# q and k' turned in 32x32 squares by VectorE and carried to their lanes, in place of transposing transfers

## The chip, the cores and the metric

One core of one Trainium2 chip. The metric is the device time of one execution in microseconds, the median of three runs: 465.61 us for the kernel before (465.29 to 465.65).

## The reference

A Linformer attention followed by a feed-forward layer. Batch 8, 8 heads, 1024 tokens, 64 channels a head, projected length 64:

```python
k_proj = np.einsum('ks,bhsd->bhkd', E, k)
v_proj = np.einsum('ks,bhsd->bhkd', F, v)
scores = scale * np.matmul(q, k_proj.transpose(0, 1, 3, 2))
attn = softmax(scores)                      # max subtracted, sum + 1e-09
attn_out = np.matmul(attn, v_proj)
...
x = attn_out.transpose(0, 2, 1, 3).reshape(B * S, H * D)   # 8192 x 512
h = x @ w_in                                # 512 x 2048
out = (h * (1.0 / (1.0 + np.exp(-1.702 * h)))) @ w_out     # 2048 x 512
```

## The kernel before

The 8192 tokens are worked in 16 blocks of 512, two to a batch: block j belongs to batch j // 2. TensorE multiplies with its operands standing on lanes: for the scores of a block it needs q with the 64 channels of a head on the lanes (two heads fill 128), and the projected k, called k', in the same way. q comes from memory with tokens on the lanes, so it has to be transposed; the projection gives k' with the projected index on the lanes, so it has to be transposed too.

Batch 0 is transposed on TensorE against an identity in the opening (`q_tr0`, `q_tr`, `k_tr`). From batch 1 on the kernel before lets a transfer do it. `q_dma` (L234 to L240; steps `qd`, `qda`, `qdb`) issues on SyncE's queue (SP) one transposing transfer of q_sb into qT for a whole batch, or half a batch in the opening; the step `kd` (L684) does the same from k_b into kt. k_b is the copy of k' out of PSUM (`kb`, L682).

The two matmuls of the feed-forward layer are each done in 7 products of half size instead of 8 (Winograd's form of Strassen's scheme): steps `u0` to `u3` make the first (L610), with sums of halves on VectorE (`xs`, `d1`, `d2`) and gelu on ScalarE (`g11` and so on, L626); `F1` to `F7` make the second (L504), from sums `gs` of the gelu outputs (L374), with copies `Fc`, `Fo` and sums `Fd` to the output tile. Eight PSUM banks are shared by all of it by a fixed plan.

The order of the work is written out by hand as words. `OPEN` lists the opening up to block 4, `STEPS` is one steady step j (run for j = 4 to 12), `TAIL` the end. A word `sc.1+3` in STEPS is the step "scores, second half" for block j + 3, `name@n/D` in OPEN the step for block n with its copy on VectorE (D) or ScalarE (A). Each engine takes its instructions in the order in which the words come, and waits in that order. Words named in BATCH are done only for the first block of a batch.

The words that matter here: `pj` projects k and v of a batch (L674). `kb` and `vq` copy the results. `sc` makes scores (L249), `ex` their exponentials (L638), `su`, `den`, `ga`, `rc`, `sr`, `sb` the sums, their reciprocals and their spreading over lanes by transfers through DRAM (den, rc, rdr, rbc), `va` the product with v', `mv` its scaling into xT (L646). `st0`, `st1` store the output. `ld` has GpSimd (POOL) issue the loads of k and v of the next batch into their single buffers, `lq` that of q of the next batch, eight transfers into the single buffer q_sb. Both first do a tiny copy into `held` that reads a tile whose arrival shall hold the loads back: for `ld` (L677) it reads qT of the batch, for `lq` (L696) it reads rbc. In a steady step the order on SP is: gather of den, transposition of k', a store, rdr, both rbc pieces, transposition of q, the other store.

Of the kernel before, what the change touches and what calls it, by code (L numbers as in the profile page):

```python
# [17 lines left out]
def kernel(ctx, tc, q, k, v, E, F,  # L18
# [86 lines left out]
    kts = [consts.tile([P, HP, KP], BF16, name=f"kt{i}") for i in range(2)]  # L105
# [89 lines left out]
    def k_tr(k_b, p0):  # L195
        n = k_b.shape[1] // 2
        t_ps = f_tile([P, n, KP], BF16)
        for p in range(n):
            nc.tensor.transpose(t_ps[:, p, :], k_b[:, 2 * p:2 * p + 2, :].rearrange("k t d -> k (t d)"),
                                ident[:KP, :KP])  # L200
        nc.vector.tensor_copy(kts[0][:, p0:p0 + n, :], t_ps)
# [21 lines left out]
    def q_tr(g):  # L223
        def go():
            if 0 not in qT:
                qT[0] = att.tile([P, J, HP, P], BF16, name="qT")
            t_ps = f_tile([P, 2, HP, P], BF16)
            for jj in range(2):
                for p in range(HP):
                    nc.tensor.transpose(t_ps[:, jj, p, :],  # L230
                                        qt[0][:, 2 * g + jj, 2 * p:2 * p + 2, :].rearrange("s t d -> s (t d)"), ident)
            nc.vector.tensor_copy(qT[0][:, 2 * g:2 * g + 2], t_ps)
        return go

    def q_dma(b, j0=0, n=J):
        def go():
            if j0 == 0:
                qT[b] = att.tile([P, J, HP, P], BF16, name="qT")
            nc.sync.dma_start_transpose(out=qT[b][:, j0:j0 + n].rearrange("r j p s -> r (j p) s"),
                                        in_=qt[b][:, j0:j0 + n].rearrange("s j h d -> s (j h d)"))  # L240
        return go

    def eight(outs, lhsTs, rhss, w=32):


        for i, ro in ((0, (LO, HI)), (1, (HI, LO))):
            for c in range(0, KP, w):
                for ri, r in zip((LO, HI), ro):
                    nc.tensor.matmul(outs[i][r.start + c:r.start + c + w], lhsTs[i][ri, c:c + w], rhss[i][ri],  # L249
                                     start=True, stop=True)  # L250

    def scores0(u, half):
# [4 lines left out]
        eight(s_ps, [kts[0][:, 2 * u + i, :] for i in range(2)], [q0s[half][u][:, :, i, :] for i in range(2)], KP)  # L257
# [118 lines left out]
    def ffn2_ops(j):  # L376
# [8 lines left out]
        wi.5@1/D sc.1@1:5,6 sc.0@1:7,4 ex.0.0@1 ex.1.1@1 ex.0.1@1 O.2.0@0:3 O.3.0@0:2 O.2.1@0 tk.0.1@1:0 qda@2  # L385
        O.3.1@0 ex.1.0@1 tk.0.0@1:5 tr.0.1@1 tm.0.1@1 tk.1.0@1:0 tk.1.1@1:7 tr.0.0@1 tm.0.0@1 O.1.0@0:6 O.1.1@0
        O.1.2@0 xt.0@1:4 gt@6 tr.1.0@1 tk.3.0@1:1 tr.1.1@1 tm.1.1@1 O.3.2@0 O.3.3@0 tk.2.1@1:5 tk.2.0@1:7
        xc.0@1/A wi.4@1 O.1.3@0 tm.1.0@1 tr.2.0@1 xt.1@1:0 tm.2.0@1 oc.3@0/D ws.1@1 tr.3.0@1 xc.1@1/A O.0.0@0:7
        ws.0@1 O.0.1@0 O.2.2@0 tk.3.1@1:4 tr.2.1@1 tm.2.1@1 O.0.2@0 tm.3.0@1 tr.3.1@1 tm.3.1@1 oc.1@0/D xt.2@1:5
        xc.2@1/A O.0.3@0 xt.3@1:1 xc.3@1/A O.2.3@0 ws.2@1 L.5@1:0 L.0@1:6 oc.0@0/D L.15@1:2 Lg.0@1 oc.2@0/A  # L390
        Lg.5@1 gt@3 L.4@1:4 L.1@1:7 pj@2:5 Lg.4@1 L.14@1:0 kb@2/A Lg.15@1 L.11@1:1 Lg.14@1 Lg.1@1 kd@2 L.2@1:6
        L.7@1:4 ws.3@1 L.9@1:3 vx.0@2 vq.0@2/D vx.1@2 vq.1@2/D Lg.7@1 Lg.11@1 ws.4@1 qdb@2 Lg.9@1 L.6@1:5
        L.8@1:4 L.10@1:7 Lg.8@1 Lg.2@1 L.3@1:1 L.12@1:3 L.13@1:2 ws.5@1/D lq@2 Lg.10@1 Lg.3@1 Lg.6@1 Lg.12@1
        Lg.13@1 gs1.0@1 sc.1@3:3,6 sc.0@2:0,1 gs2.0@1 sc.0@3:4,7 F1.0@1:2 ex.1.1@3 ex.0.1@2 gs1.1@1 gs4.0@1
        F1.1@1 gs2.1@1 gs3.0@1 Fc1@1:1/D F5.0@1:5 ex.1.0@3 ex.0.1@3 F5.1@1 F6.0@1 ex.0.0@3 ex.0.0@2 su@3:0,6
        den.0@3/A sc.1@2:3,4 tk.0.0@2:7 F2.1@1 ex.1.0@2 tk.1.0@2:0 ex.1.1@2 Fc3@1/A den.1@3/D tr.0.0@2 tm.0.0@2
        gs4.1@1 tk.0.1@2:3 tr.1.0@2 tm.1.0@2 tr.0.1@2 tm.0.1@2 tk.1.1@2:7 tr.1.1@2 F2.0@1 tm.1.1@2 F6.1@1 s0.1@0
        tk.2.1@2:4 tk.2.0@2:0 xt.0@2:6 s0.0@0 xt.1@2:3 F3.1@1 tr.2.1@2 tr.2.0@2 xc.0@2/A tm.2.0@2 tm.2.1@2 ga@3
        gs3.1@1 tk.3.0@2:0 F3.0@1 xc.1@2/A tk.3.1@2:6 tr.3.0@2 Fc2@1/A xt.2@2:3 tm.3.0@2 xc.2@2/A tr.3.1@2
        tm.3.1@2 gt@4 Fo0@1/A rc@3 xs.0@2 Fd2@1 F7.1@1 u0.P1@2:7 u0.c1@2:5/D xt.3@2:3 u1.P5@2:6 u1.P1@2:0  # L400
        u1.c1@2:2/D F7.0@1 xc.3@2/A xs.1@2 u0.P2@2 Fd1@1 u0.P5@2:4 u0.c3@2/D sr@3 u1.P2@2 u0.P6@2 u1.P6@2 F4.0@1
        u1.c3@2/D u0.c2@2/D u1.P3@2 ld@2 u2.P1@2:3 u0.g11@2 u3.P1@2:7 xs.2@2 u1.c2@2/A qd@4 u1.P7@2 u1.d2@2
        u1.g11@2 xs.3@2 F4.1@1 u0.P3@2 u1.g12@2 u2.c1@2:0/A sb@3 u1.d1@2 u2.P2@2 u0.d2@2 Fo1@1/A u3.c1@2:6/A
        u0.P7@2 u3.P2@2 u3.P5@2:4 u2.P5@2:1 u3.P6@2 u2.P6@2 u0.d1@2 u1.g22@2 u3.c3@2/D u3.P3@2 u3.g11@2 u0.g22@2
        u0.g12@2 pj@4:7 u3.c2@2/A u2.c3@2/A gs1.0@2 u3.P7@2 u2.g11@2 u3.d2@2 u2.c2@2/D gs3.0@2 gs2.0@2 u2.P7@2
        u1.P4@2 u3.g12@2 u2.P3@2 kb@4/A u3.d1@2 u0.P4@2 kd@4 u2.d1@2 F1.0@2:3 u1.g21@2 u2.d2@2 F1.1@2 u2.g22@2
        u3.g22@2 u2.g12@2 vq.1@4/A u0.g21@2 gs1.1@2 u3.P4@2 u2.P4@2 vq.0@4/A Fc1@2:1/A u3.g21@2 u2.g21@2
        va.1@3:2,7 va.0@3:4,5 gs2.1@2 mv.1.0@3 mv.0.0@3 F6.1@2 F2.0@2 mv.0.1@3 xs.0@3 mv.1.1@3 F2.1@2 sc.1@4:4,5
        sc.0@4:2,0 F6.0@2 ex.1.1@4 xs.1@3 gs3.1@2 Fc2@2/D F5.0@2:7 st1@1 st0@1 Fo0@2/D ex.0.1@4 ex.0.0@4
        ex.1.0@4 F5.1@2 F7.1@2 sc.0@5:3,6 sc.1@5:0,5 ex.0.0@5 su@4:4,2 den.1@4/A gs4.0@2 F7.0@2 ex.0.1@5  # L410
        den.0@4/D Fc3@2/D u0.P1@3:2 u1.P5@3:3 u0.P5@3:4 ex.1.0@5 u0.c1@3:6/A u1.P1@3:0 u0.c3@3/A gs4.1@2 xs.2@3
        u0.P6@3 Fd1@2 u0.c2@3/D F3.0@2 u1.c3@3/D ex.1.1@5 gt@2 ga@4 u1.c1@3:5/D u0.P3@3 F3.1@2 Fd2@2 u1.P6@3
        gt@5 u0.d2@3 rc@4 u1.c2@3/A ld@4 u0.P2@3 xs.3@3 u1.P2@3 u0.P7@3 u0.g11@3 F4.1@2 u1.P3@3 u1.P7@3 u0.d1@3
        u0.P4@3 u2.P1@3:7 F4.0@2 u1.d2@3 su@5:4,3 sr@4 u1.g11@3 pj@6:0 u1.d1@3 sb@4 Fo1@2/D u3.P1@3:2 u1.g12@3
        u1.P4@3 den.0@5/A u1.g22@3 u0.g22@3 den.1@5/D u2.c1@3:3/A u0.g12@3 kb@6/D u2.P6@3 u0.g21@3 gs1.0@3
        gs2.0@3 u2.P5@3:1 u3.P5@3:6 u3.c1@3:4/A vq.0@6/A u2.c3@3/A u3.c3@3/D u3.P6@3 u2.P2@3 u2.c2@3/A u2.P3@3
        gs3.0@3 vq.1@6/A u3.c2@3/A u3.P3@3 u2.g11@3 lq@4 u2.d2@3 u3.P2@3 u3.g11@3 u2.P7@3 u1.g21@3 u3.d2@3
        u3.P7@3 u3.d1@3 u3.g12@3 u2.g12@3 va.0@4:2,0 va.1@4:1,6 u2.d1@3 mv.0.1@4 mv.0.0@4 u2.g22@3 u3.g22@3
        F1.0@3:5 F1.1@3 u3.P4@3 kd@6 u3.g21@3 ga@5 gs1.1@3 u2.P4@3 mv.1.0@4 u2.g21@3 Fc1@3:1/A gs2.1@3 mv.1.1@4
        u1.P1@4:7 F5.0@3:0 u1.c1@4:6/A qd@6 xs.0@4 F5.1@3 rc@5 F6.1@3 F2.1@3 F2.0@3 u1.P2@4 u1.g11@4 F6.0@3  # L420
        sc.0@6:7,3 sc.1@6:4,2 ex.1.0@6 st1@2 xs.1@4 sr@5 u1.P6@4 xs.2@4 st0@2 xs.3@4 gs3.1@3 gs4.1@3 Fc3@3/D
        sb@5 gs4.0@3 ex.1.1@6 F3.0@3 F3.1@3 u1.c2@4/A Fc2@3/D Fo0@3/D ld@6 ex.0.0@6 F7.0@3 u1.P5@4:4 F7.1@3
        u1.P7@4 u2.P1@4:7 u1.c3@4/D ex.0.1@6 u0.P1@4:2 u1.P3@4 u0.P5@4:5 u0.c1@4:3/A gt@7 Fd1@3 Fd2@3 u0.P6@4
        u1.d2@4 u3.P1@4:0 u0.c3@4/D u0.c2@4/D u3.c1@4:4/A u0.P2@4 u1.g12@4 u0.P3@4 u0.g11@4 u0.d2@4 F4.0@3
        u3.P6@4 F4.1@3 u3.P2@4 u1.d1@4 u3.c2@4/D gt@1 u3.g11@4 u0.P7@4 Fo1@3/A u0.d1@4 u1.g22@4 u0.g22@4
        u2.P5@4:2 u1.P4@4 u2.c1@4:5/D u3.P5@4:0 u3.P7@4 u3.c3@4/D u2.P6@4 u1.g21@4 u0.g12@4 u2.c3@4/A u0.P4@4
        u3.d1@4 u3.P3@4 u3.P4@4 u2.c2@4/D u0.g21@4 u2.P2@4 u3.g21@4 u2.g11@4 u3.d2@4 u2.P7@4 u2.P3@4 va.0@5:0,3
        su@6:1,4 den.0@6/A u2.d1@4 den.1@6/A u2.g22@4 mv.0.1@5 u2.d2@4 va.1@5:6,7 u2.P4@4 u3.g12@4 gs1.0@4 lq@6
        u2.g21@4 st0@3
# [368 lines left out]
```

## Time and profile before

| | |
|---|---|
| median of three runs | 465.61 us |
| the profiled execution | 464.02 us |
| its span, first to last instruction | 462.2 us |
| DVE busy | 343.6 us (74%) |
| ACT busy | 307.8 us (67%) |
| POOL busy | 82.5 us (18%) |
| transfers issued by POOL (queue 0) | 86,496 packets, 29.37 MB |
| transfers issued by SP and ACT (queue 1) | 47,108 packets, 38.90 MB |
| transposing transfers of q | 8, issue 2.0 to 10.4 us (median 7.7), landing 9.1 to 14.2 us after issue |
| transposing transfers of k' | 7, issue 1.18 to 1.52 us, landing 2.9 to 6.6 us after issue |
| loads of k, v (1 MB each as they land) | median 12.2 and 16.2 us from issue to landing |

The profile is one execution, with times in microseconds from the span's start. PE is TensorE's matmuls, DVE is VectorE, ACT ScalarE, POOL GpSimd, SP SyncE. Line numbers are those of the kernel before. In a timeline row the columns are start, time (of all merged instructions), engine, line, operation, output from input, shape, count, and in square brackets how long the engine stood idle just before and what ended that wait. In the slices each digit is the busy share of a fortieth of the span in tenths; PEclk is the clock that TensorE was granted. Time that an engine other than TensorE idles costs nothing by itself.

### The profile page before, as it was taken

The numbers are of one execution on the slowest core, as the hardware profiler recorded it, in microseconds if no ns is written. First come the engines' busy times: TensorE is split into PE (matmuls) and PEld (weight loads), VectorE is DVE, ScalarE is ACT, GpSimd is POOL, SyncE is SP. The second block draws the span as 40 slices with busy tenths as digits, with TensorE's granted clock in tenths as the row PEclk, the third lists the DMA queues.
The fourth block names the chain that finished last, engine by engine and source line by source line (L and its number), as shares of the span: only waits on it lengthen the run. The fifth ranks groups of instructions, "written<-read, shape, count | busy, mean of one in ns | idle before, by whom it ended". The sixth has DMA issues, their size and how long they took to land.

```text
span 462.2 us, 10631 instructions
## 1 busy us (share of the span) xinstructions
PE 455.6 (99%) x4378; PEld 361.9 (78%) x4378; DVE 343.6 (74%) x616; ACT 307.8 (67%) x539; POOL 82.5 (18%) x111
## 2 busy tenths in 40 slices
PE   8999999999999999999999999999999999999997
PEld 4644448877778788887888788787888888888886
DVE  4547957887785977878687876888788796977771
ACT  2665367686767967769585776958677676737462
POOL 7463107052013201041010601015000000000000
PEclk9999999999999999999999999999999999999999
DMA  9999999999999978999988987989664123242022
GB/s 167 200 187 207 182 174 156 197 241 199 148 219 254 158 145 135 223 127 157 162 152 188 156 126 143 211 158 155 138 128 116 45 79 88 94 94 92 1 91 92
DMA packets 133731, 69.19 MB, mean 150 GB/s; under 512 B 98484, under 2 KB 123060, under 8 KB 133684
## 3 DMA queue, kind: packets, MB, share of 16 engines
q0 software_dynamic: 86496, 29.37, 56.7%
q1 hardware_dynamic: 47108, 38.90, 34.5%
q8 instruction: 34, 0.56, 0.5%
q10 hardware_dynamic: 80, 0.26, 0.2%
q14 instruction: 13, 0.11, 0.1%
HBM read 72.88 MB, written 16.99 MB: 194 GB/s over the span
## 4 chain that ended last, share of the span: by engine, by line
PE 87%; DMA 8%; DVE 2%; POOL 1%; issue 1%; ACT 0%; SPq 0%; DVEq 0%; POOLq 0%; ACTq 0%
PE k_ps L504 39%; PE k_ps L610 35%; PE k_ps L249 3%; PE k_ps L550 3%; PE k_ps L556 3%; DMA v_sb<-in_v_dram 3%; PE k_ps L674 2%; DMA w_in_sb<-in_moe_w_in_dram 2%; DMA rbc<-rdr 2%; DMA rdr<-rc 1%; DVE sg L357 1%; PE k_ps L652 1%; POOL k_sb L58 0%; POOL v_sb L58 0%; PE k_ps L567 0%
## 5 line engine op out<-in xcount | busy, mean ns | idle before, releaser
L504 PEld LDWEIGHTS <-sg 128*128 128x128 bf16 x960 | 93.6, 98 | 12.0 <-issue 1.3
L610 PEld LDWEIGHTS <-late 128*128 128x128 bf16 x896 | 87.4, 98 | 11.3 <-issue 1.2
L489 DVE TENSOR_TENSOR q_even<-k_ps,q_even 128x512 f32<-128x512 f32 x112 | 74.6, 687 | 22.7 <-PE k_ps L610 21.0
L610 PE MATMUL k_ps<-xw,late 128*128 128x256 bf16 x672 | 90.2, 273 | 0.0
L504 PE MATMUL k_ps<-tw,sg 128*128 128x256 bf16 x720 | 89.1, 273 | 0.0
L626 ACT ACTIVATE gT<-k_ps 128x512 bf16<-128x512 f32 x112 | 63.8, 596 | 32.8 <-PE k_ps L610 32.2
L504 PEld LDWEIGHTS <-gT 128*128 128x128 bf16 x720 | 68.7, 98 | 15.9 <-issue 8.2
L626 ACT ACTIVATE gT<-q_even 128x512 bf16<-128x512 f32 x112 | 66.2, 630 | 19.1 <-DVE q_even L489 19.0
L610 PEld LDWEIGHTS <-w_in_sb 128*128 128x128 bf16 x672 | 65.5, 98 | 9.3 <-issue 1.7
L610 PE MATMUL k_ps<-xT,w_in_sb 128*128 128x256 bf16 x448 | 64.7, 273 | 0.5 <-DVE xT L646 0.4
L504 PE MATMUL k_ps<-w_out_sb,gT 128*128 128x256 bf16 x480 | 59.3, 273 | 0.0
L70 POOL DMA_DIRECT2D q_sb<-in_q_dram x56 | 49.0, 901 | 40.5 <-DMA qT<-q_sb 18.1
L374 DVE TENSOR_TENSOR sg<-gT 128x1024 bf16<-128x1024 bf16 x60 | 40.9, 681 | 6.6 <-ACT gT L626 3.3
L614 ACT COPY k_ps<-k_ps 128x512 f32<-128x512 f32 x40 | 23.0, 575 | 22.7 <-PE k_ps L610 20.5
L646 DVE TENSOR_TENSOR xT<-k_ps,rbc 128x512 bf16<-128x512 f32 x52 | 32.8, 683 | 3.7 <-PE k_ps L249 1.4
L489 DVE TENSOR_TENSOR o_sb<-k_ps,u_sb 128x512 f32<-128x512 f32 (+1 forms) x31 | 20.6, 668 | 19.1 <-PE k_ps L504 14.4
L638 ACT ACTIVATE expT<-k_ps 128x512 bf16<-128x512 f32 x60 | 32.4, 602 | 3.1 <-PE k_ps L249 3.0
L610 PE MATMUL k_ps<-xT,late 128*128 128x256 bf16 x224 | 33.3, 273 | 0.0
L610 PE MATMUL k_ps<-xw,w_in_sb 128*128 128x256 bf16 x224 | 31.6, 273 | 0.0
L504 PE MATMUL k_ps<-w_out_sb,sg 128*128 128x256 bf16 x240 | 30.6, 273 | 0.0
L504 PE MATMUL k_ps<-tw,gT 128*128 128x256 bf16 x240 | 29.1, 273 | 0.0
L618 DVE COPY q_even<-k_ps 128x512 f32<-128x512 f32 x37 | 25.2, 683 | 5.2 <-PE k_ps L610 5.1
(122 smaller groups left out, 522.3 us busy)
## 6 DMA issues: line engine op xcount, KB each, us to landing
out_dram<-o_sb SPq DMA_DIRECT2D x30, 512.0 KB, 5.0
rbc<-rdr SPq DMA_DIRECT2D x26, 512.0 KB, 6.2
k_sb<-in_k_dram POOLq DMA_DIRECT2D x7, 1024.0 KB, 12.3
q_sb<-in_q_dram POOLq DMA_DIRECT2D x56, 128.0 KB, 6.6
v_sb<-in_v_dram POOLq DMA_DIRECT2D x7, 1024.0 KB, 17.5
w_in_sb<-in_moe_w_in_dram POOLq DMA_DIRECT2D x8, 256.0 KB, 11.3
w_out_sb<-in_moe_w_out_dram POOLq DMA_DIRECT2D x4, 512.0 KB, 11.5
v_sb<-in_v_dram POOLq DMA_DIRECT2D x4, 256.0 KB, 10.4
```

The lines of the kernel that those rows point to most:

```text
L70: nc.gpsimd.dma_start(out=qt[b][:, j], in_=qv[:, j])
L249: nc.tensor.matmul(outs[i][r.start + c:r.start + c + w], lhsTs[i][ri, c:c + w], rhss[i][ri], start=True, stop=True)
L374: nc.vector.tensor_tensor(t[i - 1], in0, in1, op=ALU.add if i == 1 else ALU.subtract)
L489: nc.vector.tensor_tensor(out_, in0, in1, op=ALU.add)
L504: nc.tensor.matmul(dst, x[:, k_, t * P:(t + 1) * P], w[:, k_], start=(first and k_ == 0), stop=(final and k_ == FH - 1), skip_group_check= ...
L550: nc.tensor.matmul(live[f"O{n}", j], gts[j][:, fc, n * P:(n + 1) * P], w_out_sb[:, fc, :], start=(fc == 0), stop=(fc == FC - 1))
L610: nc.tensor.matmul(live[h, j][:, r], a[:, k_, f:f + P], w[:, k_], start=(i in (1, 5) and r == 0 and k_ == 0), stop=(i in (2, 3, 4) and r = ...
L614: copy(new(B_, [P, 2, TH]), live[A, j])
L618: copy(u2, live[G, j])
L626: nc.scalar.activation(out_, in_, AF.Gelu_apprx_sigmoid)
L638: nc.scalar.activation(expT[j][:, 2 * n + t, :], live[f"S{n}{t}", j], AF.Exp, scale=scale)
L646: nc.vector.tensor_tensor(x_of(j)[:, n, :], live[f"V{p[1]}{t}", j], rbc[j][:, n, :], op=ALU.mult)
```

## The change

The transposing transfers go. For each block from 2 on, `q_blocks` (words `qz.0` to `qz.3`) has VectorE transpose every 32x32 square of q_sb for one group of 128 tokens, each within its own 32 lanes, into a tile qz; `q_move` (word `qx`) then carries the squares to their lanes by 16 plain transfers on SP, one for each pair of a source lane group r and a target lane group g, 32 lanes by 512 elements each. For k' of a batch, `kz` transposes squares and `kx` carries them in 8 transfers (for batch 1 seven, and one copy by POOL). qT is now a tile of one block, not of one batch, and its tokens lie in runs of 32; the scores read it so. Batch 0 keeps its way on TensorE, with k' in a tile of its own.

```diff
-    def q_dma(b, j0=0, n=J):
-        def go():
-            if j0 == 0:
-                qT[b] = att.tile([P, J, HP, P], BF16, name="qT")
-            nc.sync.dma_start_transpose(out=qT[b][:, j0:j0 + n].rearrange("r j p s -> r (j p) s"),
-                                        in_=qt[b][:, j0:j0 + n].rearrange("s j h d -> s (j h d)"))
-        return go
+    def q_tile():
+        return att.tile([P, 4, HP, JB, 32], BF16, name="qT")
+
+    def k_lhs(b, p):
+        return lambda ri, c, w: kts[b % 2][ri, c // 32, p] if b else kt0[ri, p, c:c + w]
...
+    def q_rhs(j, p):
+        return qT[j][:, :, p, :] if j == 1 else qT[j][:, :, p].rearrange("q r n s -> q n r s")
+
+    qz = {}
+
+    def q_blocks(j, n):
+        if n == 0:
+            qz[j] = att.tile([P, 4, HP, JB, 32], BF16, name="qz")
+        b, c = divmod(j, NB2)
+        nc.vector.transpose(qz[j][:, :, :, n].rearrange("s g p k -> s p g k"),
+                            qt[b][:, c * JB + n].rearrange("s (p t) (u k) -> s p (t u) k", t=2, u=2))
+
+    def q_move(j):
+        qT[j] = q_tile()
+        z = qz.pop(j)
+        for r in range(4):
+            for g in range(4):
+                nc.sync.dma_start(out=qT[j][32 * g:32 * g + 32, r], in_=z[32 * r:32 * r + 32, g])
...
         elif i == "ld":
-            nc.gpsimd.tensor_copy(held[:, 1], qT[b][:1, J - 1, 0, :1])
+            nc.gpsimd.tensor_copy(held[:, 1], rbc[j - 2][:1, 0, :1] if j - 2 in rbc else qT[max(qT)][:1, 3, 0, 0, :1])
...
-        elif i == "kd":
-            nc.sync.dma_start_transpose(out=kts[b % 2], in_=tmps["kb"].rearrange("k h d -> k (h d)"))
+        elif i == "kz":
+            tmps["kz"] = att.tile([KP, 4, HP, 32], BF16, name="k_z", bufs=1)
+            nc.vector.transpose(tmps["kz"].rearrange("s g p k -> s p g k"),
+                                tmps["kb"].rearrange("s (p t) (u k) -> s p (t u) k", t=2, u=2))
+        elif i == "kx":
+            for r in range(2):
+                for g in range(4):
+                    src, dst = tmps["kz"][32 * r:32 * r + 32, g], kts[b % 2][32 * g:32 * g + 32, r]
+                    if (b, r, g) == (1, 0, 0):
+                        nc.gpsimd.tensor_copy(dst, src)
+                    else:
+                        nc.sync.dma_start(out=dst, in_=src)
...
-    BATCH = ("qd", "pj", "kb", "kd", "vq", "ld", "lq")
+    BATCH = ("pj", "kb", "kz", "kx", "vq", "ld", "lq")
```

In the lists the other words keep their order. Where the new words stand in a steady step (in braces what goes):

```
F1.0 pj+4 ... ga+2 sc.1+3 sc.0+3 kb+4 ... gs2.1 Fc1 {kd+4} kz+4 kx+4 ex.1.1+3 ... rc+2 sr+2 u0.P1+1 sb+2 {qd+4} ld+4
{lq+3} u0.c1+1 ... F7.1 Fc3 qz.0+4 u2.P2+1 Fd1 qz.1+4 u0.P6+1 ... F4.1 F4.0 u1.P4+1 qz.2+4 Fo1 ... u2.P7+1 u3.P3+1
gs1.0+1 qz.3+4 qx+4 lq+3 u3.c2+1 u3.P2+1 ... va.0+2 ... su+3 ... va.1+2 den.0+3 den.1+3 u3.g12+1 st0
```

In the opening list `qda@2`, `kd@2` and `qdb@2` give way to `qz.0@2` to `qz.3@2`, `qx@2`, `kz@2`, `kx@2` right behind `ws.3@1`, and to `qz.0@3` to `qz.3@3`, `qx@3` right behind `ws.5@1`, ahead of `lq@2` and of `sc.1@3`. For blocks 4 and 5: `qz.3@4 qx@4` behind `u2.c2@2`, `kz@4 kx@4` behind `u1.g21@2`, `qz.3@5 qx@5 lq@4` behind `gs1.1@2`, all ahead of `sc.1@4 sc.0@4` and `sc.0@5 sc.1@5`; `ld@4` stands behind these and its hold reads qT of block 5. For block 6 `kz@6 kx@6` and then `qz.2@6 qz.3@6 qx@6` stand around `va@4`, and for block 7 `qz.3@7 qx@7 lq@6` behind `gs1.0@4`, the last words of the list but two.

## The prediction

> **What bounds the kernel now.** I read first the page's busy shares and its slices, then who TensorE waits for.
>
> ```profile
> PE 455.6 (99%) x4378; PEld 361.9 (78%) x4378; DVE 343.6 (74%) x616; ACT 307.8 (67%) x539; POOL 82.5 (18%) x111
> ...
> PE   8999999999999999999999999999999999999997
> DVE  4547957887785977878687876888788796977771
> ...
> PEclk9999999999999999999999999999999999999999
> ```
>
> TensorE is busy 99% of the span, in every slice but the first and last, and its granted clock stays at the top. DVE has a quarter of the span left. The table by 10 us stages puts all of TensorE's 6.6 idle us at 0-40 us (2.8), 120-140 (0.48), 380-390 (0.07) and the end (3.3). What it waits for:
>
> ```profile
> PE k_ps L144 <- DVE u_sb L109: 1.5, 1, 1.5
> PE k_ps L610 <- DVE xT L646: 0.4, 1, 0.4
> PE k_ps L184 <- DMA v_sb<-in_v_dram: 0.4, 1, 0.4
> PE k_ps L295 <- DVE vx L210: 0.3, 1, 0.3
> PE k_ps L184 <- DMA k_sb<-in_k_dram: 0.2, 1, 0.2
> ```
>
> These are five short waits, 2.8 us together, and none names qT or kt in the steady part. A steady pair of blocks takes 53.8 us (264.1 to 317.9). So the transposing transfers stand on nobody's path, and taking them away has at most the 0.5 us of 120-140 to win. The question is only whether the new path delivers qT in time. The third view is therefore the transfers that SP issues (count, min/median/max ns of the issue), by tile, rdr and then rc:
>
> ```profile
> L669 SPq DMA_DIRECT2D rbc<-rdr x26: 598/612/659, 92.9 to 406.9; - x26
> L665 SPq DMA_DIRECT2D rdr<-rc x13: 326/332/338, 81.7 to 404.8; - x13
> ```
>
> ```profile
> L273 SPq DMA_DIRECT2D rc<-den x13: 576/587/707, 75.5 to 398.0; - x13
> ...
> DMA to landing us min/median/max: 1.4/1.4/2.2
> ```
>
> An issue occupies SP, and issues come one after another (both rbc pieces: 1.27-1.28 us, twice 612 ns). No plain transfer costs SP less than 326 ns. The landing line is that of rc<-den: 1.4 us from issue.
>
> **What is removed.** 8 transposes of q and 7 of k', which hold SP 56 and 8.9 us (sums of the SP timeline) and load the DMA engines. Gain on the path: 0 to 0.5 us.
>
> **What is added on DVE.** 56 square transposes of q (4 a block, blocks 2 to 15) and 7 of k'. No row shows one. Nearest are a 128x512 bf16 product out of SBUF (xw, 395-412 ns) and a copy out of PSUM (683 ns); I take 0.6, for k' 0.5: 37 us in all. They lie in idle time. In a steady block the DVE timeline has waits of 1.33 and 0.72 us exactly where the third and fourth go; the first two push work that is caught up by the 1.33. Cost on the path 0; without cover up to 2.4 us a block.
>
> **What is added on SP.** 16 transfers a block (32 lanes by 1 KB) make 224, k' another 55. Their price is the main choice. Ends: 332 ns (rdr, out of SBUF into DRAM, 128 lanes) and 612 ns (rbc, into SBUF). I take 587 ns: rc<-den is the only plain transfer from SBUF to SBUF in the trace, and the load of E (64 lanes, into SBUF) has 583. The Trainium skill speaks the other way: "DMA: Bandwidth & Descriptors", section on the anatomy of one DMA, gives some 50 ns for the sequencer's dispatch, and its section on issuing engines calls issue time usually small. By it, a block's squares would be there after 15 x 0.05 + 1.4 = 2.2 us; by the rdr row 15 x 0.332 + 1.4 = 6.4; by the rc row 15 x 0.587 + 1.4 = 10.2, with SP held 9.4 us (k': 4.7). The rows decide. The scores of a block read all lanes and all parts of qT, so they wait for the last.
>
> How long there is, in a steady block: the fourth transpose stands behind gs1.0 on DVE and ahead of the next wait.
>
> ```profile
> 285.84 0.68 DVE L374 TENSOR_TENSOR sg<-gT 128x1024 bf16<-128x1024 bf16 x1
> 287.25 0.69 DVE L489 TENSOR_TENSOR q_even<-k_ps,q_even 128x512 f32<-128x512 f32 x1 [0.72 <-PE k_ps L610]
> ```
>
> ```profile
> 290.90 1.05 PE L504 MATMUL k_ps<-w_out_sb,gT 128*128 128x256 bf16 x8
> 291.88 0.62 PE L249 MATMUL k_ps<-qT,kt 64*32 64x512 bf16 x16
> ```
>
> gs1.0 ends at 286.5, the transpose at 287.1, and the scores start at 291.9: 4.8 us. When k and v are projected in between (1.85 us, even blocks' projections, ahead of odd blocks' scores) it is 319.7 - 313.1 = 6.6. Needed are 10.2. TensorE works in order, so all behind the scores waits too. gs1.0 sits behind DVE waits on TensorE and so moves with it: the loss recurs.
>
> Blocks 8, 10, 12, 14, and 15 (no projection any more): 10.2 - 4.8 = 5.4 each, 27. Blocks 9, 11, 13: 10.2 - 6.6 = 3.6 each, 10.8. Block 7 has the same place at the end of the opening list: gs1.0 ends at 156.5, ready 157.1 + 10.2 = 167.3, scores at 158.2: 9.1.
>
> Blocks 2 and 3 share SP in the opening:
>
> ```profile
> 60.17 0.43 DVE L691 CAST vx<-k_ps 64x256 bf16<-64x256 f32 x1 [3.04 <-ACT k_b L682]
> ...
> 63.95 1.22 DVE L335 CAST tw<-rbc 128x2048 bf16<-128x2048 f32 x1
> 68.03 0.69 DVE L374 TENSOR_TENSOR sg<-gT 128x1024 bf16<-128x1024 bf16 x1 [2.85 <-ACT gT L559]
> ```
>
> ```profile
> 69.02 0.84 PE L249 MATMUL k_ps<-qT,kt 64*32 64x512 bf16 x24
> ```
>
> The first four transposes fit the 3.04 us wait (57.1 to 59.5), the four of block 3 the 2.85 us (65.7 to 68.1, k' having cost 0.5). But SP issues block 2 until 68.9, k' (7) until 73.0, and block 3 is ready at 83.2: 14.2 us late for 69.0.
>
> The rest of the opening, each time counted as if the losses before it were taken out:
> Block 4: squares ready on DVE at 95.8; SP issues them to 105.2, then k' of this batch, ready 110.7; scores at 104.1: 6.6. Block 5: SP goes on from 109.9, ready 120.1; scores at 108.3 + 6.6: 5.2.
>
> **The moved loads.** The hold on POOL ahead of k and v of batch 3 now names block 5's qT; before it ran at 96.8, now at 120.1. Issue 0.3 + 0.9, v landing 16.2 (median of its loads): 137.5. The projection stands at 120.0 + 11.8: 5.7. In steady blocks the hold names rbc of two blocks earlier, which lands near 30% of a block, as early as before: 0. The q loads move behind the fourth transpose of odd blocks, start near 313 instead of 311 and land by about 326; the next batch's first transpose, behind Fc3, comes near 332: 0.
>
> Block 6: k' on SP from 127.0 to 131.7, ready 141.9; scores at 137.3: 4.6.
>
> Behind SP's squares stand den's gather, rdr, rbc and the stores. The gather goes out at 322.9 instead of 317.9, but its reader on DVE (325.9) moves with the stalled scores to 329.5, so 5 us are left after a 1.4 us landing; where v is loading the gather takes some 7.5 us (issued 291.9, awaited to 299.7) and 0.7 us is left: 0. On DVE a transpose waits for q's load and for the squares of two blocks back, both long done. The moving operand of the scores now comes in runs of 32 elements; the projections (runs of 64) still take 215 ns for 512 columns, so 0, at most double, 14 x 0.56 = 7.8.
>
> Sum: 27 + 10.8 + 9.1 + 14.2 + 6.6 + 5.2 + 5.7 + 4.6 = 83.2.
>
> **The clock.** TensorE has no idle stretch over 1.5 us between its first and last matmul, and its clock stays at 1.00. "TensorE: Matmul & The Clock Gate", section on the HAM clock gate, says that an idle window of 3.4 us halves it until a busy one has passed. By the trace alone 0; by the page, a stall of s us holds a whole window with chance (s - 3.4)/3.4, summed over the eleven stalls over 3.6 us 7.4, each 1.7 us: 12.6. I take the page, as no row is near. Against the profiled run's 464.0 (span 462.2): 464.0 + 83.2 + 12.6 = 559.8; the median lies 1.6 above that run: 561, forecast 560.
>
> **Rivals.**
> First, cheap issue, 332 ns (for: the floor of all rows; against: no row into SBUF has it). The same places: block 3 5.5, 4 and 5 1.9, loads 5.7, block 7 5.3, five times 1.6; others fit. 26.4, with 3 for the clock: 495.
> Second, dispatch as on the page: block 3 1.3 (ready on DVE only at 68.1), loads 0.3, block 7 1.1: 468.3.
> Third, not slower: the transposing transfers leave the DMA engines, the rbc transfers of block 4 (5.8 and 7.0 us) land sooner and the 0.5 us at 120-140 closes: 465.1. It decides only if squares land within 4.8 us (issue under 0.21 us) and block 3's scores are less than 0.9 us late. Against it: the floor of 326 ns. That the change doesn't do what it says I leave out: the built order shows 63 square transposes and no transposing transfer.
>
> **How the numbers follow.** The 587 ns case 0.60 (540 to 585: landings slower beside k and v loads by up to 3 us at three blocks, DVE cover, scores' reads; below, the clock), cheap issue 0.25 (490 to 510), page's dispatch 0.10, not slower 0.05. Range 490 to 585. A measurement of this kernel tells 0.2% (0.9 us) from no change; of the last 0.05 I give 0.02 to faster, 0.03 to same; slower 0.95.
>
> **What would show it.** SP rows of the squares near 590 ns, sixteen in a row for over 9 us; TensorE waiting on the squares at every scores group, 3.5 to 5.5 us in steady blocks, with its clock dipping; one wait on v's load near block 6; DVE without new waits. It is wrong if the issues are far under 0.33 us, or if the scores wait for something else, DVE above all.

## The result, and the profile after

The changed kernel takes 609.32 us (median of four runs, 607.48 to 610.49); the kernel before, beside it, 465.63 (465.29 to 466.92). The ratio is 1.308, with an interval of 1.303 to 1.312: a third slower, where the prediction had 560 and a range up to 585. The profiled execution took 610.49 us, its span is 608.7.

From the page of the changed kernel, the busy shares, and of the slices TensorE and its clock:

```profile
PE 492.8 (81%) x4372; PEld 375.1 (62%) x4378; DVE 380.8 (63%) x679; ACT 308.4 (51%) x539; POOL 83.2 (14%) x112
...
PE   8999539944984929779596896959779695999997
...
PEclk9999959977995978969799897989979797899999
```

TensorE is busy 492.8 us where it was 455.6, with the same work: 37.2 more, at a mean granted clock of 0.899. It stands idle 608.7 - 492.8 = 115.9 us where it was 6.6: 109.3 more. Together 146.5, which is what the span grew by. Whom TensorE waits for (us in total, times, longest):

```profile
PE k_ps L270 <- DMA qT<-qz: 87.9, 18, 15.2
PE k_ps L270 <- DVE o_sb L548: 8.5, 1, 8.5
PE k_ps L270 <- DMA kt<-k_z: 6.1, 3, 5.2
```

Nearly all is waiting at L270, the scores: 103.6 us in all, most of it for the squares on their way from qz to qT. The rest is 4.5 us of waits on DVE and 1.2 on ACT that the kernel before did not have. The tile's own rows (count, min/median/max ns), and last the scores of the kernel before:

```profile
L262 SPq DMA_DIRECT2D qT<-qz x224: 507/589/1785, 59.8 to 513.6; - x112
L270 PE MATMUL k_ps<-qT,kt x224: 376/606/631, 84.6 to 515.9; 64*32 64x512 bf16 x112
...
DMA to landing us min/median/max: 1.8/2.5/5.8
```

```profile
L249 PE MATMUL k_ps<-qT,kt x240: 372/376/387, 37.0 to 371.9; 64*32 64x512 bf16 x120
```

An issue takes SP 589 ns, as the row rc<-den had said. A scores matmul takes 376 ns at its fastest, which is the median of the kernel before, so its new median of 606 is not the price of reading in runs of 32. One steady block (block 9), on DVE, SP and TensorE. The columns are start, time, engine, work and the wait before it:

```profile
286.74 0.70 DVE L254 STREAM_TRANSPOSE qz<-q_sb 128x512 bf16<-128x512 bf16 x1
```

```profile
287.53 11.44 SPq L262 DMA_DIRECT2D qT<-qz  x16
```

```profile
300.31 1.51 PE L270 MATMUL k_ps<-qT,kt 64*32 64x512 bf16 x16 [6.21 <-DMA qT<-qz]
301.75 1.89 PE L528 MATMUL k_ps<-w_out_sb,gT 128*128 128x256 bf16 x8
```

The fourth transpose ends at 287.4, SP issues sixteen transfers until 299.0, the last one lands, and the scores start at 300.3, 6.2 us after TensorE ran dry. Behind the wait, eight matmuls take 1.89 us; in the kernel before the group behind such scores took 1.05:

```profile
320.27 1.05 PE L504 MATMUL k_ps<-w_out_sb,gT 128*128 128x256 bf16 x8
```

The same place in windows of 2 us (start:end, length, TensorE's busy time, matmuls, granted clock, DMA share, GB/s):

```profile
294.00:296.00 2.00, 0.10 (x2) 1.00 2.07 165
...
304.00:306.00 2.00, 2.00 (x12) 0.50 0.06 12
...
308.00:310.00 2.00, 2.00 (x20) 1.00 0.04 8
```

The clock is at 1.00 while TensorE runs dry (294.1), at half from some 2 us later (0.54 in 296 to 298), still at half 4 to 6 us after the restart, and then back. The trace has 13 such spells of half clock, one at the wait of each block from 3 to 15. The first of them as a window, and the sum over all 13:

```profile
74.29:91.36 17.07, 6.14 (x44) 0.50 1.09 130
...
sum 122.90, PE 67.52; mean PE 5.19
```

TensorE worked 67.5 us at half clock. At full clock that work would take half as long, so by this estimate the clock cost 33.8 us, 2.6 for each wait (1.7 to 3.3). The other 3.4 of the 37.2 us are not the clock's; what they are stays open (e11 below, at a mean clock of 1.000, is busy 2.5 us longer than before, too).

### The profile page after: what moved, and what is told of

The parts are those of the page before. It is cut to its first block, busy times and chain, and to the rows that moved or that the text cites. A ratio compares the mean times of both kernels' runs of the same rounds, so it can differ in the third digit from the quotient of the medians.

```text
span 608.7 us, 10993 instructions
## 1 busy us (share of the span) xinstructions
PE 492.8 (81%) x4372; PEld 375.1 (62%) x4378; DVE 380.8 (63%) x679; ACT 308.4 (51%) x539; POOL 83.2 (14%) x112
## 4 chain that ended last, share of the span: by engine, by line
PE 56%; SPq 20%; DMA 12%; DVE 7%; issue 4%; ACT 0%; POOL 0%; DVEq 0%; POOLq 0%; ACTq 0%
PE k_ps L528 27%; PE k_ps L634 21%; SPq L262 17%; DMA qT<-qz 8%; PE k_ps L270 3%; PE k_ps L336 2%; SPq L718 2%; DMA q_even<-in_q_dram 2%; DVE qz L254 2%; DMA rc<-den 1%; PE k_ps L574 1%; DVE sg L395 1%; DVE q_even L640 1%; DMA out_dram<-o_sb 1%; DVE rbc L360 1%
## 5 line engine op out<-in xcount | busy, mean ns | idle before, releaser
L528 PEld LDWEIGHTS <-sg 128*128 128x128 bf16 x960 | 95.8, 100 | 17.8 <-DVE sg L395 2.5
L270 PE MATMUL k_ps<-qT,kt 64*32 64x512 bf16 x224 | 22.1, 605 | 103.6 <-DMA qT<-qz 87.9
L634 PE MATMUL k_ps<-xw,late 128*128 128x256 bf16 x672 | 93.1, 278 | 0.9 <-DVE xw L387 0.9
L528 PE MATMUL k_ps<-tw,sg 128*128 128x256 bf16 x720 | 92.2, 279 | 0.0
L528 PEld LDWEIGHTS <-gT 128*128 128x128 bf16 x720 | 74.0, 105 | 25.2 <-issue 12.6
L270 PEld LDWEIGHTS <-kt 64*32 64x32 bf16 x224 | 4.1, 99 | 114.2 <-DMA qT<-qz 62.0
L528 PE MATMUL k_ps<-w_out_sb,gT 128*128 128x256 bf16 x480 | 70.7, 306 | 0.0
L634 PE MATMUL k_ps<-xT,w_in_sb 128*128 128x256 bf16 x448 | 68.8, 284 | 1.0 <-DVE xT L670 0.9
L542 ACT COPY k_ps<-k_ps 128x512 f32<-128x512 f32 x13 | 7.4, 572 | 84.4 <-PE k_ps L528 83.0
L638 ACT COPY k_ps<-k_ps 128x512 f32<-128x512 f32 x40 | 23.0, 574 | 36.1 <-PE k_ps L634 35.1
L254 DVE STREAM_TRANSPOSE qz<-q_sb 128x512 bf16<-128x512 bf16 x56 | 38.4, 697 | 0.0
```

What stands on the lines that cost most here:

```text
L254: nc.vector.transpose(qz[j][:, :, :, n].rearrange("s g p k -> s p g k"), qt[b][:, c * JB + n].rearrange("s (p t) (u k) -> s p (t u) k", t= ...
L528: nc.tensor.matmul(dst, x[:, k_, t * P:(t + 1) * P], w[:, k_], start=(first and k_ == 0), stop=(final and k_ == FH - 1), skip_group_check= ...
L634: nc.tensor.matmul(live[h, j][:, r], a[:, k_, f:f + P], w[:, k_], start=(i in (1, 5) and r == 0 and k_ == 0), stop=(i in (2, 3, 4) and r = ...
```

## The experiments

| run | us | to before (interval) | TensorE busy, us | idle, us |
|---|---|---|---|---|
| before | 465.6 | 1 | 455.6 | 6.6 |
| changed | 609.3 | 1.308 (1.303 to 1.312) | 492.8 | 115.9 |
| e9_twice_the_issues | 751.6 | 1.614 (1.609 to 1.618) | 492.4 | 257.4 |
| e10_half_the_bytes | 606.2 | 1.302 (1.299 to 1.304) | 490.8 | 112.0 |
| e2_via_dram | 572.1 | 1.227 (1.223 to 1.231) | 487.0 | 83.9 |
| e7_two_queues | 596.4 | 1.280 (1.276 to 1.284) | 490.1 | 106.1 |
| e6_stores_act | 606.2 | 1.301 (1.298 to 1.305) | 491.5 | 112.4 |
| e3_dummies | 594.1 | 1.276 (1.271 to 1.281) | 523.2 | 68.8 |
| e1_early_steps | 550.5 | 1.182 (1.177 to 1.187) | 477.7 | 74.2 |
| e8_early_two_queues | 496.7 | 1.067 (1.064 to 1.069) | 467.8 | 27.0 |
| e4_k_only | 483.6 | 1.038 (1.034 to 1.041) | 461.0 | 19.3 |
| e5_no_carry | 481.8 | 1.035 (1.031 to 1.039) | 459.0 | 19.5 |
| e12_kv_first | 479.6 | 1.031 (1.028 to 1.033) | 460.6 | 16.0 |
| e11_dve_added | 473.9 | 1.017 (1.015 to 1.020) | 458.1 | 14.6 |

Idle is the span less the busy time. My theory: the sixteen issues of a block stand in a row on SP between its fourth transpose and its scores, and each wait that they make also costs clock. The rivals: bytes and landings, DVE, the way qT is read, the k' path.

### Number of issues or bytes: e9, e10

First e9's edit (32 issues, the same bytes), then that of e10 (16 issues, half the bytes):

```diff
-                nc.sync.dma_start(out=qT[j][32 * g:32 * g + 32, r], in_=z[32 * r:32 * r + 32, g])
+                for h in range(2):
+                    nc.sync.dma_start(out=qT[j][32 * g:32 * g + 32, r, 2 * h:2 * h + 2],
+                                      in_=z[32 * r:32 * r + 32, g, 2 * h:2 * h + 2])
...
+                nc.sync.dma_start(out=qT[j][32 * g:32 * g + 32, r, :2], in_=z[32 * r:32 * r + 32, g, :2])
```

> As the changed kernel, but each transfer of q's squares is cut into two of half its bytes: 32 issues a block in place of 16, the same bytes at the same places. Theory (the number of issues on SP, some 0.6 us each, is the cost): 16 x 0.6 = 9.6 us more for each block, on the path of 13 waits and twice at block 3: 610 + 14 x 9.6 = 744; 720 to 770. Rival (bytes, landings or the loads beside them set it): 605 to 625.

> As the changed kernel, with all 16 transfers a block at their places, but each carries only the first half of its row (this leaves out q of heads 4 to 7, whose scores read the q of heads 0 to 3). Theory (number of issues): 600 to 610, as the full bytes, with at most the 1 us a block that the issues take longer beside loads gained. Rival (bytes): the 10 to 11.7 us of a block halve, 13 waits fall by about 5, and the clock's share with them: 520 to 550.

751.6 and 606.2 us. SP's row of qT in the first, then in the second:

```profile
L263 SPq DMA_DIRECT2D qT<-qz x448: 507/589/1542, 60.0 to 655.7; - x150
```

```profile
L262 SPq DMA_DIRECT2D qT<-qz x224: 507/589/1333, 59.6 to 509.2; - x112
```

The price of an issue is 589 ns with 1 KB a lane and with 512 bytes. Twice the issues add 141.5 us of idle time to TensorE, 10.1 for each of 14 blocks; half the bytes take away 4. The theory holds within 8 us, and bytes are ruled out as the main cause. One more thing stands in the table: with its waits more than doubled, e9 has the same busy time, 492.4. It has 13 spells of half clock too, in which TensorE worked 65.6 us, against 67.5. Between these two kernels the clock's price goes with the number of waits and not with their length.

### Fewer issues, by way of DRAM: e2

```diff
-        for r in range(4):
-            for g in range(4):
-                nc.sync.dma_start(out=qT[j][32 * g:32 * g + 32, r], in_=z[32 * r:32 * r + 32, g])
+        d = dram.tile([P, 4, HP, JB, 32], BF16, name="qdr")
+        nc.sync.dma_start(out=d, in_=z)
+        for g in range(4):
+            nc.sync.dma_start(out=qT[j][32 * g:32 * g + 32].rearrange("s r p n k -> s r (p n k)"),
+                              in_=d.rearrange("(r s) g p n k -> s r g (p n k)", r=4)[:, :, g])
```

> Places as in the changed kernel, but a block's squares go to DRAM in one transfer and come back in four, so 5 issues in place of 16 and twice the bytes. Theory (number of issues): SP is held 0.33 + about 2 for the first landing + 4 x 0.6 = 4.7 us in place of 10 to 11.7, the last part lands about 7 us after the fourth transpose in place of 12; each of 13 waits falls by about 5 us, block 3's by 10: 104 falls to about 30 us, the clock's 37 to about 8: 506. Rival (bytes and landings beside the loads set it, not issues): 600 to 625.

572.1 us: 37 gained where I expected 103. SP in two blocks, an even and an odd one:

```profile
307.00 0.33 SPq L261 DMA_DIRECT2D qdr<-qz  x1
314.41 1.78 SPq L263 DMA_DIRECT2D qT<-qdr  x4
...
342.15 0.33 SPq L261 DMA_DIRECT2D qdr<-qz  x1
344.84 1.75 SPq L263 DMA_DIRECT2D qT<-qdr  x4
```

The issues themselves fell as expected, to 0.33 + 1.8 us. But the way now has two landings, and the first took 7.1 us in the even block (307.33 to 314.41), where v is being loaded, and 2.4 in the odd one. Waits of 6 to 7 us remain at blocks 8, 10 and 12, and 3 to 5 at 9, 11 and 13; at 14 and 15, where no load runs any more, they are 2.0 and 1.7. I had priced a landing beside loads like one without.

### Two queues at the old places: e7

```diff
-                nc.sync.dma_start(out=qT[j][32 * g:32 * g + 32, r], in_=z[32 * r:32 * r + 32, g])
+                (nc.scalar if r % 2 else nc.sync).dma_start(out=qT[j][32 * g:32 * g + 32, r], in_=z[32 * r:32 * r + 32, g])
```

> As the changed kernel, but every second group of the squares of q is issued on ACT's queue, so 8 issues on SP and 8 beside them on ACT for each block, all at the old places. Theory (one queue's serial issue is the limit): the last square lands some 5 us sooner; after what the way through DRAM gave (landings grow beside loads), 13 waits fall by 3.5 to 5 us, block 3's by up to 10, and with them most of the clock's share: 515 to 550. Rival 1 (the transfers share one resource behind the queues): 600 to 610. Rival 2 (ACT's own work is held up by its waits for the squares and by 5 us of issues a block): over 550 with new waits for ACT.

596.4 us. At eight blocks TensorE now waits elsewhere (its largest wait):

```profile
PE k_ps L634 <- ACT q_even L640: 53.9, 8, 8.7
```

At block 10 ACT issues its eight transfers in 8.8 us and only then makes the copy that TensorE needs for the next feed-forward products. At block 15 SP's eight take 5.3:

```profile
314.53 8.83 ACTq L262 DMA_DIRECT2D qT<-qz  x8
323.40 0.59 ACT L640 COPY q_even<-k_ps 128x512 f32<-128x512 f32 x1 [9.10 <-DMA qT<-qz]
```

```profile
493.71 5.28 SPq L262 DMA_DIRECT2D qT<-qz  x8
```

Rival 2 has it: the wait moved to ACT. As for rival 1, at blocks 14 and 15, with no load running, both queues were through in 5.3 us, where the changed kernel took 10.1 and 11.0: there they work side by side. At block 10, beside v's load, SP's eight took 9.1 us against 10.9 for sixteen on one queue. One issue keeps its 0.6 there, but between two of ACT's lies a pause of 3.3 us that no row explains, so beside loads the share of rival 1 stays open.

### The stores: e6

```diff
-                nc.sync.dma_start(out=ov[:, 2 * g:2 * g + 2], in_=outs.pop((j, g)))
+                eng_ = nc.scalar if j == 1 else nc.sync
+                eng_.dma_start(out=ov[:, 2 * g:2 * g + 2], in_=outs.pop((j, g)))
```

In the changed kernel, block 5's scores wait 8.5 us for DVE. SP at that time, and DVE:

```profile
131.87 11.22 SPq L262 DMA_DIRECT2D qT<-qz  x16
143.19 1.00 SPq L568 DMA_DIRECT2D out_dram<-o_sb  x2
```

```profile
148.73 0.69 DVE L548 COPY o_sb<-k_ps 128x512 f32<-128x512 f32 x1 [10.40 <-DMA out_dram<-o_sb]
```

DVE's copy into o_sb cannot start before the stores of the previous contents, and these stand behind 8 and 16 issues.

> As the changed kernel, but the two output stores of block 1 are issued by ACT, not behind the squares on SP. Theory (block 5's wait of 8.5 us is DVE's copy that waits for these two stores; behind it the squares of block 5, landed 4 us after TensorE stopped, are next): 4 to 5 us gained, 1 to 2 of clock with it: 603 to 605. Rival (the wait returns elsewhere, at block 6): 608 to 610.

606.2 us, 3.2 less, though the intervals of the two ratios overlap. Block 5's wait is now 3.1 us (2.4 and 0.7), and for the squares: 5.4 us less, of which 1.9 came back elsewhere (idle time fell by 3.5). The trace shows the mechanism; its price in time is near the spread, and smaller than I gave it.

### The clock: e3

```diff
+            if t == 1 and j >= 7:
+                for _ in range(24):
+                    nc.tensor.matmul(s_ps[0], zeros[:, :P], zeros, start=True, stop=True)
             eight(s_ps, [k_lhs(b, 2 * t + e) for e in range(2)],
```

> Ahead of each scores group of blocks 7 to 15, which is where TensorE waits 5.4 to 11.4 us, TensorE makes 24 matmuls of zeros (5.2 us) into the bank that the scores then overwrite; nothing else is changed. Theory (37 us of extra busy time are the clock that falls while TensorE stands still): the waits are partly filled at no cost and 9 of 13 parts of the 37, 26 us, go: 583. Rival (the matmuls are slow for another reason): 609. If the waits were shorter than the fill: above 609.

594.1 us, a gain of 15.2 by making TensorE do 216 useless matmuls. Its clock by slices, and two places as windows:

```profile
PEclk9999959987897897999999999999999899999999
```

```profile
259.34:262.75 3.41, 2.28 (x10) 1.00 0.19 51
262.75:266.16 3.41, 2.60 (x34) 1.00 0.81 304
464.14:467.55 3.41, 1.58 (x21) 1.00 0.31 102
467.55:470.96 3.41, 3.41 (x29) 0.50 0.68 256
```

Behind block 7 the clock stays up, but for 3.4 us at block 14 (467.55 to 470.96). The dummies took 5.35 us a block, 48.1 in all, and the idle time fell by 47.1: they cost nothing. Busy time without them is 523.2 - 48.1 = 475.1, 17.7 less than in the changed kernel: 2.5 for each of the seven waits of blocks 8 to 15 that no longer halve the clock. My 26 took all of the 37 for the clock's and nine spells for gone. With nothing but idle time filled, TensorE's own work became faster: the clock follows the waits.

### Earlier, and on two queues: e1, e8

In e1 only words of the steady step move: `qz.0+4` behind `kx+4`, `qz.1+4` behind `F2.0`, the others with `qx+4` and `lq+3` to `u1.d2+1`, half a step earlier.

```diff
-  u0.c1+1 xs.2+1 F5.1 u1.P3+1 gs3.0 Fc2 gs4.1 u0.c3+1 u0.P2+1 u1.c2+1 u1.d2+1 gs4.0 ...
-  gs1.0+1 qz.3+4 qx+4 lq+3 u3.c2+1
+  u0.c1+1 xs.2+1 F5.1 u1.P3+1 gs3.0 Fc2 gs4.1 u0.c3+1 u0.P2+1 u1.c2+1 qz.2+4 u1.d2+1 qz.3+4 qx+4 lq+3 gs4.0 ...
+  gs1.0+1 u3.c2+1
```

> The steady steps' square transposes and their sixteen transfers are put some 11 us earlier (blocks 8 to 15), and the loads of q behind them; the opening list is untouched. Theory (a block's sixteen issues, 10 to 11.7 us, stand in a row between its fourth transpose and its scores; the clock falls only because TensorE stands still): the waits of blocks 8 to 15 go, 53 us by their rows, and with them 8 of 13 parts of the 37 us by which TensorE's busy time grew, 23: 609 - 76 = 533. Rival 1 (the matmuls are slow for another reason than the waits, such as the way qT lies or transfers beside them): only the 53 go, 556. Rival 2 (DVE pays once the transposes stand away from its waits, up to 2.4 us a block): 552 at most.

550.5 us. Of the 53 us of waits in blocks 8 to 15, 10 are left, all at even blocks, where SP first issues k' and then takes 12 to 13 us for the sixteen beside the loads of k and v. Busy time fell by 15.1 with them. The total lies between theory and rival 1, but the spells of half clock settle it: 8 are left of 13, TensorE worked 39.2 us in them instead of 67.5, and half of the difference, 14.1, is nearly all of the 15.1. Rival 1 is out. The wait left at block 8 is short, 2.15 us, and stands alone. TensorE's clock around it in e1:

```profile
257.50:259.50 2.00, 0.15 (x8) 1.00 1.13 309
260.50:263.50 3.00, 3.00 (x16) 0.50 0.32 126
264.00:266.00 2.00, 2.00 (x21) 1.00 0.00 0
```

It stood still from 257.2 to 259.35 and was then granted half the clock for some 3.4 us (in windows of 0.5 us, from 260.4 to 263.8), while it was busy. So a wait far under 3.4 us can cost clock, too. Whether it does is not a matter of its length alone: in e3 two waits of 1.00 and 0.83 us at block 14 were followed by half clock, and two of 1.06 and 0.88 at block 8 were not (the windows there), nor was one of 2.79 us in e5. The spells' own times show why. All traces together have 100 of them, and each lasts 3.41 us or a whole multiple of it. Laid out on this raster, e5's wait falls on two windows with 1.4 us each; that of e1 falls into one:

```profile
124.04:127.45 3.41, 2.04 (x22) 1.00 1.20 193
127.45:130.86 3.41, 1.99 (x17) 1.00 0.46 126
130.86:134.28 3.42, 3.42 (x33) 1.00 0.96 189
```

```profile
256.97:260.38 3.41, 1.26 (x21) 1.00 1.16 300
```

In the twelve traces that have such spells, every one of the 92 full-clock windows with 2.0 us or more of idle time was followed by half clock, none of the 1,547 with under 1.55, and 8 of the 22 between. At half clock it came back after each of the 94 windows with under 0.3 us of idle time, and after none of the 180 with over 0.8.

e8 moves the opening's words forward as well, lets POOL issue every second group of squares, and puts the loads behind them.

```diff
-                nc.sync.dma_start(out=qT[j][32 * g:32 * g + 32, r], in_=z[32 * r:32 * r + 32, g])
+                (nc.gpsimd if r % 2 else nc.sync).dma_start(out=qT[j][32 * g:32 * g + 32, r], in_=z[32 * r:32 * r + 32, g])
```

> The square transposes and transfers of all blocks put as early as q's load allows (opening too), half of each block's squares on SP and half on POOL's queue, loads of q and k, v behind them. Theory (only lateness costs, bytes and DVE do not): no wait in the steady steps, in the opening 5 to 20 us with the clock: 472 to 492. Rival (a floor of contention by 279 more transfers, on landings or on DVE, remains): above 500.

496.7 us. TensorE over a steady pair of blocks (columns as above):

```profile
276.00:330.06 54.06, 53.90 (x546) 1.00 0.98 158
```

54.06 us for the pair (54.14 for the next), where the kernel before takes 53.8, at the full clock: in the steady step the new path costs nearly nothing once it starts early enough. The eight on POOL take 4.0 us beside SP's eight in 5 to 7.6; the Trainium skill, "DMA: Bandwidth & Descriptors", section "Issuing engines are not separate DMA queues", says that a second issuing engine saves issue time only, and issue time was what was to be saved. Nearly all of the 31 us over before lies in the opening, just past my expectation: by the rows 7.2 us of waits on k', some 10 on DVE, 2.9 on squares, and by the four spells of half clock 8.4 for the clock. I see no placing that would beat the kernel before, where TensorE had only 6.6 us of idle time.

### DVE and k' alone: e11, e5, e12, e4

e11 adds the change's transposes to the kernel before at the change's places, results unused, with the loads of q behind them as in the change (a steady step is below); e5 is the change without the carrying:

```diff
- F7.1 Fc3 u2.P2+1 Fd1 u0.P6+1 ... F4.0 u1.P4+1 Fo1 ... gs1.0+1 u3.c2+1
+ F7.1 Fc3 qz.0+4 u2.P2+1 Fd1 qz.1+4 u0.P6+1 ... F4.0 u1.P4+1 qz.2+4 Fo1 ... gs1.0+1 qz.3+4 lq+3 u3.c2+1
```

```diff
-        qT[j] = q_tile()
-        z = qz.pop(j)
...
-                nc.sync.dma_start(out=qT[j][32 * g:32 * g + 32, r], in_=z[32 * r:32 * r + 32, g])
+        qT[j] = qz.pop(j)
```

> The kernel before with its transposing transfers, to which VectorE's 63 square transposes are added at the places of the changed kernel, with their results unused; the loads of q stand behind them as in the change. Theory by what the kernel without the carrying showed (new short waits on DVE in the opening, none in the steady steps): 8 us of waits and 2 of clock, 472 to 478. Rival, as predicted (DVE hides all): 465 to 467. If more: q's loads, now behind the transposes, come too late for the transposing transfers: above 480.

> The changed kernel without the 224 transfers of q: the scores read VectorE's square transposes where they lie (this leaves out carrying the squares to their lanes; all instructions of TensorE, DVE and ACT and the reads in runs of 32 stay, and so does the k' path). Theory (the 224 issues on SP are the cost; DVE's 63 transposes and the reads in runs of 32 cost nothing): 466 to 472, the few us for k' transfers at block 4. Rival 1 (DVE's 39 us more stand in the way): 480 to 505. Rival 2 (reads in runs of 32 are slower): 14 x 0.56 = 8 us more, 474 to 480.

473.9 us, 8.3 over before, where I had predicted that all would hide; the waits lie in the opening. TensorE's waits in e11 that before did not have:

```profile
PE k_ps L682 <- DMA v_sb<-in_v_dram: 2.2, 1, 2.2
PE k_ps L618 <- DVE q_even L497: 2.2, 2, 1.6
```

So 2.2 of the 8.3 us are a wait on v's load, which stands on POOL behind the q loads and so behind the transposes; the others are waits on DVE or on ACT.

e5 took 481.8 us, 10 over my theory and in the range of rival 1, but only by the opening. Behind 168 us into its span TensorE waits 1.1 us in all, so neither the steady transposes nor the reads in runs of 32 cost anything; ahead of that there are the waits on DVE and 2.8 us on v at the projection of batch 3. POOL in e5:

```profile
104.57 7.00 POOL L70 DMA_DIRECT2D q_sb<-in_q_dram  x8 [10.39 <-DVE sg L391]
111.51 0.17 POOL L697 CAST held<-qz 1x1 f32<-1x1 bf16 x1
111.64 0.89 POOL L58 DMA_DIRECT2D k_sb<-in_k_dram  x1
```

The hold (L697), which I had named as the cause, did not wait at all. k and v stand behind the q loads, and these had waited for DVE until 104.6, where block 5's last transpose ended at 104.0. e12 puts k and v first (`ld@4` ahead of `lq@4`, held by block 4):

```diff
- qz.3@5 qx@5 lq@4 u3.P4@2
+ qz.3@5 qx@5 ld@4 lq@4 u3.P4@2
...
-            nc.gpsimd.tensor_copy(held[:, 1], rbc[j - 2][:1, 0, :1] if j - 2 in rbc else qT[max(qT)][:1, 3, 0, 0, :1])
+            nc.gpsimd.tensor_copy(held[:, 1], rbc[j - 2][:1, 0, :1] if j - 2 in rbc else qT[j][:1, 3, 0, 0, :1])
```

> As the kernel without the carrying of q (so the scores again read the squares where they lie, which leaves out the carrying), with the loads of k and v of batch 3 put ahead of the loads of q on POOL's queue and held by block 4 in place of block 5. Theory (the wait of 2.8 us for v at the projection of batch 3 comes from POOL's order: k and v stand behind the q loads, which stand behind block 5's square transposes): that wait goes, 478 to 480. Rival (what the prediction named: the loads are late because of their hold alone): the same gain, but in the kernel without the carrying the hold would have been seen to wait, and it did not. Third (q then comes later and block 6 waits for it): 481 to 484.

479.6 us (478.4 to 481.0, against 480.3 to 483.4 in e5): the wait on v is gone, 2.4 us came back as waits on k', and the gain of 2.2 us is near the spread.

e4 has the new path for k' alone, in the kernel before, with the functions of the change:

```diff
- gs2.1 Fc1 kd+4 ex.1.1+3
+ gs2.1 Fc1 kz+4 kx+4 ex.1.1+3
```

> The kernel before with the new path for k' alone (square transpose and 8 transfers at the places where the transposing transfer stood); q keeps its transposing transfers. Theory (k' stands early in a step, with some 20 us to its scores, so its 4.7 us of issues hide): 465 to 468. Rival (the 6.1 us that TensorE was seen to wait for kt, with their clock, belong to the k' path itself): 472 to 478.

483.6 us, over both theories. SP at block 6:

```profile
138.26 5.00 SPq L701 DMA_DIRECT2D kt<-k_z  x8
...
144.25 4.90 SPq L240 DMA_TRANSPOSE qT<-q_sb  x1
```

Eight issues of k' stand ahead of the gather and of q's transposing transfer, which block 6's scores then await for 6.5 us; block 4 waits 3.5 for k'. Behind that the steady steps show no wait on kt or qT. I had thought of the readers of k', not of what is queued behind it; and at block 6 `kz` stood later on DVE than the change has it, so I take e4 for the upper end for k'; that is argued, not shown.

## Why the prediction was too low

The route was right: TensorE waits at the scores of every block from 3 on, for sixteen issues in a row, and its clock suffers. Two terms of the sum failed in size, and nearly all of the miss is theirs: the time from the transposes to the scores, and the clock. Against the profiled run the sum was 50.7 us short (559.8 to 610.5). The waits at the scores were 103.6 us instead of 77.5, 26.1 more; the clock took 33.8 instead of 12.6, 21.2 more; another 3.4 of busy time are unexplained. The 5.7 for the moved loads did not come, but 5.7 of small waits on DVE and ACT did: that these two cancel is luck.

- **Price of an issue: right.** 587 ns taken, 589 measured, with 1 KB and with 512 bytes (e10). The 50 ns that the prediction weighed against it are no rival price: "DMA: Bandwidth & Descriptors", section "Anatomy of one DMA — SWDGE (gpsimd) path", gives them for the dispatch alone, on POOL's path, and there too an issue took 498 ns (e8).
- **From the transposes to the scores: failed in size.** 10.2 us predicted, 12.9 measured at block 9. Sixteen issues took 10.0 to 10.1 us at seven blocks, but 10.6 to 11.7 at the other seven, most of which had loads of q, k or v beside them. Landings took 1.8 to 5.8 us (median 2.5), not 1.4. So blocks 8 to 15 waited 53 us, not 38; blocks 9, 11 and 13 were most off, 6.0 to 6.5 instead of 3.6.
- **The opening.** Block 3 waited 15.9 us (14.2 predicted), block 4 7.2 (6.6), block 6 7.6 (4.6), block 7 11.4 (9.1): the squares and, at blocks 4 and 6, k' beside them on SP.
- **"Behind SP's squares ... the stores ... 0": failed.** At block 5 the wait was 8.5 us (5.2 predicted, for the squares), because the stores hold DVE's copy; without them it is 3.1 (e6).
- **The moved loads, 5.7: failed.** In the changed kernel no wait names them; I take it that the earlier waits give them time. Without those they cost 2.8, by POOL's order, not by the hold (e5, e12).
- **DVE at nothing: failed in the opening, held in the steady steps.** 8.3 us with the q loads behind it (e11); a transpose took 0.70 us, not 0.6. In the changed kernel 4.5 us of waits on DVE are left.
- **The scores' reads: right, 0** (376 ns, and e5).
- **The clock: failed in size, in both factors.** The prediction had 7.4 halvings of 1.7 us each; measured are 13 of 2.6. The price: half clock lasts until a busy window has passed, as the prediction says itself. TensorE restarts somewhere inside a window, so the rest of that one and a whole one go at half clock, 3.4 to 6.8 us, and half of that is lost: 1.7 to 3.4. The prediction took the least. The number: it asked for a wholly idle window, for which the measured waits give a chance of 11 in all (an estimate by its own formula), where its shorter waits gave 7.4; and 2.0 us of idle time in a window are enough (e1), so every wait of this kernel counted. "TensorE: Matmul & The Clock Gate", "HAM oscillation — how this bites in real kernels", describes this case: each wait over one window, met at every tile, is paid at every tile; here 13 of 13.

What stays open: what stretches sixteen issues from 10 us to 11 or 12 (and to 13 in e1). Loads alone it is not: blocks 7 and 11 took 10.1 beside q's loads, and block 15 took 11.0 with none running. Open is also where 3.4 us of TensorE's busy time come from.

## What to carry to other kernels

Replacing one transfer by sixteen is paid on the queue of the engine that issues: multiply the count by the issue time of the nearest row of the same kind, and ask whether the sum fits between the data's last write and its reader. If TensorE bounds the kernel and waits even some 2 us in each step, add a price for its clock to each wait, here 1.7 to 3.3 us whether the wait was 5 or 15 (and 2.7 at 34, e9). And when a queue gets longer, list everything behind it: here stores held a copy in PSUM, and k' held q.

## What the runs showed of the hardware

An issue on SP from SBUF to SBUF takes 589 ns with 1 KB and with 512 bytes for each of 32 lanes (e9, e10), much the same on ACT's queue (601, e7); POOL's eight took 4.0 us (e8). Two queues issued sixteen in 5.3 us where one took 10.1 to 11.0, with no load beside them (e7, blocks 14 and 15). A write of 512 KB from SBUF to DRAM landed after 2.4 us, and after 7.1 while v was loaded (e2).

In these traces TensorE's clock changed on a raster of 3.41 us, by what the window before had held. Behind a window with 2.0 us or more of idle time it was halved (92 of 92), behind one with under 1.55 never, and it came back behind each with under 0.3 (94 of 94). "TensorE: Matmul & The Clock Gate", section on the HAM clock gate, speaks of an idle window of about 3.4 us: the window's length agrees, but it need not be idle as a whole (e1: 2.15 us).
